# Batch 1's values loaded in two halves around q and k of batch 2, and batch 2's first transposes moved up

## The chip, the cores and the metric

The kernel runs on one core of a Trainium2 chip. The core has five engines, each with its own instruction stream: TensorE (PE; its weight loads are listed apart as PEld), VectorE (DVE), ScalarE (ACT), GpSimd (POOL) and SyncE (SP). They meet only at semaphores. Transfers between DRAM and the on-chip memory are done by 16 DMA engines; POOL and SP issue nearly all of them here, and the instructions of the engines arrive by DMA too. The metric is device time in microseconds (us), the median of several runs. The kernel before takes 302.07 us (three runs, 301.28 to 302.17).

## What is computed

Global-local attention for 8 batches of 8 heads, 512 local and 32 global tokens with head dimension 64, and then a two-layer network on the 4352 resulting rows of 512 numbers:

```python
s_g = scale * q_g @ concat(k_g, k_l).T
out_g = softmax(s_g) @ concat(v_g, v_l)
s_ll = where(abs(i - j) <= 32, scale * q_l @ k_l.T, -1e9)
s_lg = scale * q_l @ k_g.T
out_l = softmax(concat(s_lg, s_ll)) @ concat(v_g, v_l)
x = concat(out_g, out_l)          # per batch and head, then heads side by side: [4352, 512]
h = x @ w_in                      # [512, 2048]
out = (h * sigmoid(1.702 * h)) @ w_out
```

All inputs and the output are float32; the kernel casts to bf16 as it loads.

## The kernel before

*Tiling.* Heads are worked on four at a time. Such a group is a "quad": batch b has quads 2b (heads 0 to 3) and 2b + 1 (heads 4 to 7). In the code around the change `a` is the first quad of a batch and `c` the second. Local tokens are laid out as 16 by 32 positions. The local scores of a quad are computed for five overlapping chunks of keys (`PARTS`, `FIRST`), in two rounds (`rnd` 0 and 1), each round filling a pair of PSUM tiles from `spair()`.

*Steps of a quad* (class `Wide`, on top of `Quad`). `Tk` and `Tq` turn the loaded k and q (tiles `rk` and `rq` in `loaded[b]`) by a VectorE transpose into `kT` and `q`. `kcopy` and `qcopy` make second copies of parts of them. `ext` puts the global q and k next to the local ones; its four parts can run on VectorE, or on ScalarE if `on_act` is given. `transpose_g` turns the global q and k of some quads. `S(rnd)` is the score product on TensorE (L557), `X(rnd)` the exponential on ScalarE (L568), `M(rnd)` the product with the band mask (L573), on VectorE unless POOL is given. `U(0)` sums the exponentials through a matrix of ones, `U(1)` and `U(2)` multiply them with the two halves of the values (L583), `Gm` does the global rows (L594). `R` turns the sums and takes reciprocals (L459 to L463), `XL` scales and writes `xL`, the input of the network (L468), and `G` finishes the global rows.

*The network.* `h_mm` is the first product (L612, 64 matmuls of 512 columns a batch), `h_act` the activation: tanh on ScalarE (L619) and one VectorE instruction (L620) that writes `gT`. For four of the sixteen tiles of batch 1 this goes in two pairs (L829, L830). `o_mm` is the second product (L637); every fourth one ends in `o_out`, which copies PSUM to `ob` on ScalarE (L651) and stores it by four DMAs from SP (L659).

*Order.* The schedule is written out by hand: each engine executes its instructions in the order of the program text. The program does batch 0's attention, then batch 0's first product, then (L763 on) the second product of batch 0 with batch 1's attention strewn in, then batch 1's first product (L811 to L855), then `phase_o(1)`, the second product of batch 1 with the rest of batch 2's attention, and so on in the same pattern for batches 2 to 7. Batch 2's quad `a` is prepared during batch 1's first product: its transposes, copies and `ext` at `fc` 1 to 6, its first scores at `fc` 10.

*Loads.* Nearly all loads are issued by POOL, in program order, between POOL's own work. `load_rest` (L250) issues the values of batch 0, the weights, q and k of batch 1, and at its end the values of batch 1 (`load_v(1)`, five DMAs, one for each chunk of keys, over all eight heads), half of q of batch 2 and the global q and k of quads 4 to 7 (`load_g(4, 8)`). Then POOL does `a.M(0)` of batch 1 (L775), issues all of k and the other half of q of batch 2 (L776, L777), does `c.M(0)` (L789) and issues the values of batch 2 and q and k of batch 3. Eight semaphores serve POOL's loads in turn, so each issue waits until the load eight places earlier has landed. The global rows of batch 1's values are loaded once (`load_vg1`) and copied to three more places on ScalarE by `copy_vg1` (L105; L778).

*Names.* L is the line number. `loaded[2][0]` is k and `loaded[2][1]` q of batch 2; the second index `[:, u]` takes one quad's half.

Of the kernel before, what the change touches and what calls it, by code (L numbers as in the profile page):

```python
# [20 lines left out]
def kernel(  # L21
# [12 lines left out]
    nc = tc.nc  # L34

    B, H, Sl, D = q_l.shape
# [29 lines left out]
    qf = q_l.rearrange("b (u j) (r t) d -> b (j r) u (t d)", j=4, t=16)  # L66
    kf = k_l.rearrange("b (u j) (r t) d -> b (j r) u (t d)", j=4, t=16)
# [4 lines left out]
    loaded = {}  # L72

    def load(b, us=(0, 1), kq=True):
        if b not in loaded:
            loaded[b] = (ld.tile([128, 2, 16 * D], BF16, name="rk"),
                         ld.tile([128, 2, 16 * D], BF16, name="rq"))
        if kq:
            s = slice(us[0], us[-1] + 1)
            nc.gpsimd.dma_start(out=loaded[b][1][:, s], in_=qf[b][:, s])  # L80
            nc.gpsimd.dma_start(out=loaded[b][0][:, s], in_=kf[b][:, s])
# [3 lines left out]
    FIRST = (0, 96, 192, 320, 416)  # L85

    def v_view(b, n):
        return vtiles[b % 2][:, : 8 * n * (D + 2)].rearrange("p (u j c d) -> p u j c d", u=2, j=4, c=n)

    def load_v(b):  # L90
        if b == 2:
            nc.gpsimd.memset(v_view(b, 5)[:, :, :, :, D:], 1.0)
        vt = v_view(b, 5).rearrange("p u j c d -> p (u j) c d")
        vs, vg = (x[b].rearrange("h s d -> s h d") for x in (v_l, v_g))
        for c in range(5):
            n = 128 if c == 2 else 96
            nc.gpsimd.dma_start(out=vt[0:n, :, c, :D], in_=vs[FIRST[c] : FIRST[c] + n])  # L97
            if c != 2 and b != 1:
                nc.gpsimd.dma_start(out=vt[96:128, :, c, :D], in_=vg)  # L99

    def load_vg1():
        vt = v_view(1, 5).rearrange("p u j c d -> p (u j) c d")
        nc.gpsimd.dma_start(out=vt[96:128, :, 0, :D], in_=v_g[1].rearrange("h s d -> s h d"))

    def copy_vg1():  # L105
        vt = v_view(1, 5).rearrange("p u j c d -> p (u j) c d")
        src = vt[96:128, :, 0:1, :D]
        on_act(vt[96:128, :, 1:2, :D], src)
        on_act(vt[96:128, :, 3:5, :D], src.to_broadcast([32, 8, 2, D]))

    def on_act(out_, in_):
        nc.scalar.activation(out_, in_, AF.Copy)  # L112
# [11 lines left out]
    def load_g(lo, hi, names="kq"):  # L124
        for name, dst, src in (("k", rkg, kgf), ("q", rqg, qgf)):
            if name in names:
                nc.gpsimd.dma_start(out=dst[:, lo:hi, :], in_=src[:, lo:hi, :])
# [37 lines left out]
    for i in range(2):  # L165
# [3 lines left out]
        out=step, in_=step, pattern=[[1, 289]], compare_op=ALU.is_ge,  # L169
# [51 lines left out]
    def make_mask(part):  # L221
        rnd, at, t0, t1, nr, base, rows = part
        src = band[:, base : base + 16 * nr].rearrange("p (r t) -> p t r", t=16)
        nc.gpsimd.tensor_copy(mask_at(rnd, at, t1 - t0, nr)[0:rows], src[0:rows, t0:t1])
# [13 lines left out]
    def transpose_g(lo, hi, names="qk"):  # L238
        for name, dst, s in (("q", qgT, rqg), ("k", kgT, rkg)):
            if name not in names:  # L240
                continue
            nc.vector.transpose(dst[:, lo:hi, :32], s[:, lo:hi].bitcast(F32))

    def load_v2(b):
        vp = v_l[b].rearrange("(u h) (c p) d -> u p h c d", u=2, p=128)
        for u in range(2):
            for p in (slice(0, 64), slice(64, 128)):
                nc.gpsimd.dma_start(out=v_view(b, 4)[p, u, :, :, :D], in_=vp[u, p])

    def load_rest():  # L250
        load_v2(0)
        n = d_ff // 4
        for part in range(4):
            if part == 3:
                for m in MASKS:
                    make_mask(m)
            for u in range(2):
                nc.gpsimd.dma_start(out=w_in_sb[:, part, 2 * u : 2 * u + 2],
                                    in_=w_in_r[u][:, :, part * n : part * n + n])
        for g4 in (1, 0, 2, 3):  # L260
            nc.gpsimd.dma_start(
                out=w_out_sb[:, 4 * g4 : 4 * g4 + 4, :].rearrange("p (g e) m -> p g (e m)", e=2),
                in_=w_out_r[:, 2 * g4 : 2 * g4 + 2, :])
            if g4 == 0:
                load(1, (0,))
                load_g(2, 4)
                load_vg1()
            if g4 == 2:
                load(1, (1,))
        load_v(1)  # L270
        load(2, kq=False)
        nc.gpsimd.dma_start(out=loaded[2][1][:, 0], in_=qf[2][:, 0])
        load_g(4, 8)

    xG = consts.tile([128, NKC, B * Sg], BF16)
    xL = {}
# [328 lines left out]
    def width(i):  # L605
        return TB if i < B else B * Sg
# [3 lines left out]
    def h_mm(i, fc, hp, kcs):  # L610
        for kc in kcs:
            nc.tensor.matmul(hp[:, : width(i)], lhsT=w_in_c[:, fc // 4, kc, fc % 4 // 2, :, fc % 2],  # L612
                             rhs=(xL[i] if i < B else xG)[:, kc, :],
                             start=(kc == 0), stop=(kc == NKC - 1))

    def h_act(i, fc, hp):
        n = width(i)
        th = moe.tile([128, TB], F32, name="th", bufs=4)
        nc.scalar.activation(th[:, :n], hp[:, :n], AF.Tanh, scale=0.851)  # L619
        nc.vector.scalar_tensor_tensor(gTs[i][:, fc, :n], in0=th[:, :n], scalar=1.0,  # L620
                                       in1=hp[:, :n], op0=ALU.add, op1=ALU.mult)

    def h_step(i, fc):
        if fc == 0:
            gTs[i] = moe.tile([128, FC, TB], BF16, name="gT")
        hp = pbank("hp")
        h_mm(i, fc, hp, range(NKC))
        h_act(i, fc, hp)

    def o_mm(i, st):  # L630
        tci, f4 = divmod(st, 4)
        first = (i, tci) not in ops
        if first:
            ops[i, tci] = pbank("op")
        op = ops[i, tci]
        for fc in range(4 * f4, 4 * f4 + 4):
            nc.tensor.matmul(op, lhsT=gTs[i][:, fc, tci * 128 : tci * 128 + 128],  # L637
                             rhs=w_out_sb[:, fc, :], start=(first and fc == 4 * f4), stop=(fc == FC - 1))
        if f4 == 3:
            o_out(i, tci, op)  # L640
# [27 lines left out]
    a, c = Quad(0), Quad(1)  # L668
# [90 lines left out]
    def osteps(i, *sts):  # L759
        for tci, f4 in sts:  # L760
            o_mm(i, 4 * tci + f4)

    nq = {1: (Wide(2), Wide(3)), 2: (Wide(4), Wide(5))}  # L763
    a, c = nq[1]
    transpose_g(2, 4)
    a.Tk(False)
    a.Tq(False)
# [4 lines left out]
    osteps(0, (0, 1), (0, 0), (1, 1), (1, 0), (2, 1), (2, 0))  # L772
    a.S(0)
    a.X(0)
    a.M(0, nc.gpsimd)  # L775
    nc.gpsimd.dma_start(out=loaded[2][0], in_=kf[2])  # L776
    nc.gpsimd.dma_start(out=loaded[2][1][:, 1], in_=qf[2][:, 1])  # L777
    copy_vg1()  # L778
    c.Tk()
    c.Tq()  # L780
    c.ext()
    osteps(0, (0, 2), (1, 2), (2, 2))
    a.S(1)
    a.X(1)
    a.M(1)
    osteps(0, (0, 3), (1, 3))
    c.S(0)
    c.X(0)
    c.M(0, nc.gpsimd)  # L789
    load_v(2)  # L790
    load(3)
    osteps(0, (2, 3), (3, 0))
    c.S(1)
    c.X(1)
    for unit in range(3):
        a.U(unit)
    a.R()
# [15 lines left out]
    for kcs in ((0, 1), (2,), (3,)):  # L813
        for fc in range(4):
            h_mm(1, fc, hps[fc], kcs)
    a.G()
    c.G()
    pt = spair()
# [3 lines left out]
    a, c = nq[2]  # L822
    for fc in range(FC):
        if fc < 4:
            h_act(1, fc, hps[fc])
        elif fc in (4, 6):
            f = slice(fc, fc + 2)
            th, ps = early[:, fc - 4 : fc - 2], pt[1 - (fc - 4) // 2]
            nc.scalar.activation(th, ps, AF.Tanh, scale=0.851)  # L829
            nc.vector.scalar_tensor_tensor(gTs[1][:, f, :], in0=th, scalar=1.0, in1=ps,  # L830
                                           op0=ALU.add, op1=ALU.mult)
        elif fc >= 8:
            h_step(1, fc)
        if fc == 1:
            transpose_g(4, 6)
            a.Tk(False)
        if fc in (2, 3):
            a.ext((fc - 2,), on_act)
        if fc == 3:
            a.Tq(False)  # L840
        if fc == 4:
            a.kcopy(on_act)
            a.ext((2,), on_act)
        if fc == 6:
            a.ext((3,), on_act)
            a.qcopy(on_act)
        if fc == 10:
            a.S(0)
            a.X(0, (0,))
        if fc == 11:  # L850
            a.X(0, (1,))
            a.M(0, nc.gpsimd)
            load_v(3)
            load(4)
            load_g(8, NQ)  # L855
# [109 lines left out]
```

## Time and profile before

| what | value |
|---|---|
| median of three runs | 302.07 us |
| the profiled execution | 303.67 us, of which 302.0 us from the first to the last instruction (the span) |
| mean granted TensorE clock | 0.994 of full speed |
| one batch in the regular part (from batch 2 to batch 3) | 33.0 us |
| second product of batch 0 with batch 1's attention | 32.3 to 55.0 us |
| first product of batch 1 | 55.0 to 72.4 us |
| bytes moved by DMA, mean rate | 28.19 MB, 93 GB/s |
| DMA rate in 20 to 40 us / 65 to 75 us | 202 / 3 GB/s |

How to read the lines of the profile: an instruction's row has engine, line, operation, the tiles it writes and reads, the shapes, and the count. In a timeline the first number is the start, the second the length, both in us, and the bracket says how long the engine stood idle ahead of it and what released it; "issue" means that nothing the profile shows held it. In the chain of waits the two numbers are start and length of each piece. A DMA issue is listed with its size and the time from issue to landing. "DMA queue" rows give packets, MB and share of the 16 engines' time; q0 holds POOL's loads, q1 SP's stores, q8 and q14 carry instructions.

### The profile page before, as it was taken

What the parts mean: (1) busy time and instruction counts of PE and PEld (TensorE: products, weight loads), DVE (VectorE), ACT (ScalarE), POOL (GpSimd) and SP (SyncE); (2) the same over time, 40 slices, a digit from 0 to 9 for tenths busy, and PEclk for the clock granted to TensorE, in tenths of its full rate; (3) what the DMA queues carried; (4) which work ended last, traced back from release to release, by engine and by line L of the source; (5) the groups of instructions that cost most, each with busy time, mean ns of one, the idle gap of its engine ahead of it and who ended that gap; (6) DMA issues with size and microseconds to landing.
All of it is one profiled execution on the core that took longest, in us unless ns stands there. A gap on an engine that the chain in (4) does not pass through costs nothing.

```text
span 302.0 us, 8148 instructions
## 1 busy us (share of the span) xinstructions
PE 288.5 (96%) x3390; PEld 150.2 (50%) x3431; DVE 215.0 (71%) x421; ACT 173.1 (57%) x284; POOL 87.1 (29%) x131
## 2 busy tenths in 40 slices
PE   6999999799999999999999999999999999999995
PEld 6544445244554455444554455445454455446653
DVE  7678756498777878797887878797969866673320
ACT  4836695089556764476537746577357651663421
POOL 8973779607927000810054001600000000000000
PEclk9999999799999999999999999999999999999999
DMA  7999999950999711990269512900220012101113
GB/s 200 172 196 211 205 163 186 178 104 4 145 199 155 130 28 45 112 175 14 61 77 135 99 37 72 123 1 20 55 54 17 2 41 67 35 0 37 36 47 94
DMA packets 59444, 28.19 MB, mean 93 GB/s; under 512 B 47504, under 2 KB 49808, under 8 KB 59408
## 3 DMA queue, kind: packets, MB, share of 16 engines
q0 software_dynamic: 51568, 17.57, 52.6%
q1 hardware_dynamic: 7360, 9.45, 11.4%
q10 hardware_dynamic: 480, 0.66, 0.7%
q8 instruction: 27, 0.44, 0.6%
q14 instruction: 9, 0.07, 0.1%
HBM read 36.31 MB, written 8.91 MB: 150 GB/s over the span
## 4 chain that ended last, share of the span: by engine, by line
PE 85%; ACT 4%; DVE 3%; issue 2%; ACTq 0%
PE hp L612 36%; PE op L637 35%; PE ov L583 5%; PE s L557 5%; ACT e L568 2%; PE s L612 1%; DVE gT L620 1%; ACT ob L651 1%; DVE gT L830 1%; PE op L649 1%; PE og L594 1%; ACT v L112 1%; PE s L583 0%; DVE e L573 0%; DVE kT L509 0%
## 5 line engine op out<-in xcount | busy, mean ns | idle before, releaser
L637 PE MATMUL op<-w_out_sb,gT 128*128 128x512 bf16 x498 | 119.1, 379 | 2.4 <-DVE rT L461 0.7
L620 DVE SCALAR_TENSOR_TENSOR gT<-th,hp 128x512 bf16<-128x512 f32 (+1 forms) x136 | 86.8, 654 | 38.2 <-ACT th L619 38.2
L612 PE MATMUL hp<-xL,w_in_sb 128*128 128x512 bf16 x471 | 106.3, 383 | 0.6 <-issue 0.2
L619 ACT ACTIVATE th<-hp 128x512 f32<-128x512 f32 (+1 forms) x136 | 77.1, 573 | 44.7 <-PE hp L612 41.9
L612 PEld LDWEIGHTS <-w_in_sb 128*128 128x128 bf16 x576 | 56.4, 99 | 65.3 <-issue 2.4
L637 PEld LDWEIGHTS <-gT 128*128 128x128 bf16 x528 | 49.3, 98 | 55.7 <-issue 0.8
L651 ACT ACTIVATE ob<-op 128x512 f32<-128x512 f32 (+2 forms) x35 | 20.4, 588 | 66.0 <-PE op L637 63.5
L568 ACT ACTIVATE e<-s 128x1016 bf16<-128x1016 f32 (+1 forms) x56 | 53.5, 1006 | 2.0 <-PE s L557 1.9
L97 POOL DMA_DIRECT2D v<-in_v_l_dram x35 | 28.3, 815 | 82.3 <-PE og L594 81.5
L573 DVE TENSOR_TENSOR e<-e,mask 128x1712 bf16<-128x1712 bf16 (+1 forms) x25 | 27.1, 1082 | 6.0 <-ACT e L568 5.4
L459 DVE STREAM_TRANSPOSE sT<-ov 128x512 f32<-128x512 f32 x15 | 10.8, 717 | 19.5 <-PE ov L583 18.0
L468 DVE TENSOR_TENSOR xL<-ov,rs 128x512 bf16<-128x512 f32 x29 | 18.7, 685 | 1.8 <-PE ov L435 0.5
L557 PEld LDWEIGHTS <-kT 32*128 32x128 bf16 x672 | 12.8, 93 | 13.2 <-issue 9.7
L557 PE MATMUL s<-q,kT 32*128 32x160 bf16 (+1 forms) x448 | 15.0, 246 | 0.8 <-DVE gT L830 0.5
L509 DVE STREAM_TRANSPOSE kT<-rk 128x512 f32<-128x512 f32 x14 | 14.6, 1039 | 1.6 <-DMA rk<-in_k_l_dram 1.6
L99 POOL DMA_DIRECT2D v<-in_v_g_dram x24 | 14.3, 595 | 0.3 <-DMA v<-in_v_g_dram 0.3
L573 POOL TENSOR_TENSOR e<-e,mask 128x1760 bf16<-128x1760 bf16 x3 | 10.0, 3322 | 12.9 <-issue 12.2
L463 DVE STREAM_TRANSPOSE rs<-rT 128x512 f32<-128x512 f32 x16 | 11.4, 711 | 0.6
L583 PEld LDWEIGHTS <-v 128*32 128x32 bf16 x672 | 10.5, 97 | 2.4 <-issue 2.4
L583 PE MATMUL ov<-e,v 128*32 128x128 bf16 (+3 forms) x624 | 11.7, 223 | 0.0
L314 DVE STREAM_TRANSPOSE q<-rq 128x512 f32<-128x512 f32 (+1 forms) x17 | 11.2, 662 | 0.0
L612 PE MATMUL hp<-xG,w_in_sb 128*128 128x256 bf16 x64 | 9.6, 273 | 0.0
(112 smaller groups left out, 182.4 us busy)
## 6 DMA issues: line engine op xcount, KB each, us to landing
out_dram<-ob SPq DMA_DIRECT2D x132, 64.0 KB, 2.3
rk<-in_k_l_dram POOLq DMA_DIRECT2D x6, 512.0 KB, 9.6
v<-in_v_l_dram POOLq DMA_DIRECT2D x28, 96.0 KB, 4.7
rq<-in_q_l_dram POOLq DMA_DIRECT2D x5, 512.0 KB, 7.5
w_in_sb<-in_moe_w_in_dram POOLq DMA_DIRECT2D x8, 256.0 KB, 7.6
w_out_sb<-in_moe_w_out_dram POOLq DMA_DIRECT2D x4, 512.0 KB, 10.1
v<-in_v_l_dram POOLq DMA_DIRECT2D x11, 128.0 KB, 4.8
rq<-in_q_l_dram POOLq DMA_DIRECT2D x5, 256.0 KB, 9.0
```

The costliest lines, as they stand in the source:

```text
L97: nc.gpsimd.dma_start(out=vt[0:n, :, c, :D], in_=vs[FIRST[c] : FIRST[c] + n])
L468: nc.vector.tensor_mul(self.x[:, 2 * self.u + h, :], self.st[1 + h], self.st["rs"])
L509: nc.vector.transpose(flat[:, 0:Sl].rearrange("p (r t) -> p t r", t=16), loaded[self.b][0][:, self.u].bitcast(F32))
L557: nc.tensor.matmul(bank(self.ps, j)[:, at : at + n], lhsT=self.k[p, KEYS[c] : KEYS[c] + 128, e], rhs=qs[p, :, :, e], start=(e == 0), stop= ...
L568: nc.scalar.activation(self.E[rnd][:, 2 * i : 2 * i + 2, :n], self.ps[i][:, :, :n], AF.Exp, scale=scale)
L573: eng.tensor_mul(e, e, mask[:, rnd : rnd + 1, :n].to_broadcast([128, 4, n]))
L583: nc.tensor.matmul(ov[32 * j : 32 * j + 32, :].rearrange("p (t r) -> p t r", t=16)[:, t0:t1, r0 : r0 + nr], lhsT=lv, rhs=self.E[rnd][:, j, ...
L612: nc.tensor.matmul(hp[:, : width(i)], lhsT=w_in_c[:, fc // 4, kc, fc % 4 // 2, :, fc % 2], rhs=(xL[i] if i < B else xG)[:, kc, :], start=( ...
L619: nc.scalar.activation(th[:, :n], hp[:, :n], AF.Tanh, scale=0.851)
L620: nc.vector.scalar_tensor_tensor(gTs[i][:, fc, :n], in0=th[:, :n], scalar=1.0, in1=hp[:, :n], op0=ALU.add, op1=ALU.mult)
L637: nc.tensor.matmul(op, lhsT=gTs[i][:, fc, tci * 128 : tci * 128 + 128], rhs=w_out_sb[:, fc, :], start=(first and fc == 4 * f4), stop=(fc = ...
L651: nc.scalar.activation(ob[:, lo:hi], op[:, lo:hi], AF.Copy, scale=0.5)
```

## The change

`load_v` takes a range of heads. The values of batch 1 are loaded in two calls, heads 0 to 3 and heads 4 to 7 (ten DMAs of half the size in place of five). Between them stand q and k of quad 4 (the first half of batch 2) and the global q and k. The other half of q and k of batch 2 is issued after `c.M(0)` of batch 1, ahead of the values of batch 2. `a.M(0)` of batch 1 moves from POOL to VectorE and behind the preparation of `c`. `copy_vg1` moves to the start of batch 1's attention. The transposes of quad 4 (`Tq`, `Tk`) move into batch 1's attention behind `a.M(1)`, its `kcopy` and `qcopy` behind `c.X(1)`, and the global transposes ahead of `a.G()`. In batch 1's first product there remain the four parts of `ext`, one behind each of the first four tiles. The order of TensorE's instructions is the same as before.

```diff
--- before.py
+++ after.py
@@ -87,14 +87,14 @@
     def v_view(b, n):
         return vtiles[b % 2][:, : 8 * n * (D + 2)].rearrange("p (u j c d) -> p u j c d", u=2, j=4, c=n)
 
-    def load_v(b):
+    def load_v(b, hs=slice(0, 8)):
         if b == 2:
             nc.gpsimd.memset(v_view(b, 5)[:, :, :, :, D:], 1.0)
         vt = v_view(b, 5).rearrange("p u j c d -> p (u j) c d")
         vs, vg = (x[b].rearrange("h s d -> s h d") for x in (v_l, v_g))
         for c in range(5):
             n = 128 if c == 2 else 96
-            nc.gpsimd.dma_start(out=vt[0:n, :, c, :D], in_=vs[FIRST[c] : FIRST[c] + n])
+            nc.gpsimd.dma_start(out=vt[0:n, hs, c, :D], in_=vs[FIRST[c] : FIRST[c] + n, hs])
             if c != 2 and b != 1:
                 nc.gpsimd.dma_start(out=vt[96:128, :, c, :D], in_=vg)
 
@@ -267,10 +267,10 @@
                 load_vg1()
             if g4 == 2:
                 load(1, (1,))
-        load_v(1)
-        load(2, kq=False)
-        nc.gpsimd.dma_start(out=loaded[2][1][:, 0], in_=qf[2][:, 0])
+        load_v(1, slice(0, 4))
+        load(2, (0,))
         load_g(4, 8)
+        load_v(1, slice(4, 8))
 
     xG = consts.tile([128, NKC, B * Sg], BF16)
     xL = {}
@@ -762,6 +762,7 @@
 
     nq = {1: (Wide(2), Wide(3)), 2: (Wide(4), Wide(5))}
     a, c = nq[1]
+    copy_vg1()
     transpose_g(2, 4)
     a.Tk(False)
     a.Tq(False)
@@ -772,26 +773,28 @@
     osteps(0, (0, 1), (0, 0), (1, 1), (1, 0), (2, 1), (2, 0))
     a.S(0)
     a.X(0)
-    a.M(0, nc.gpsimd)
-    nc.gpsimd.dma_start(out=loaded[2][0], in_=kf[2])
-    nc.gpsimd.dma_start(out=loaded[2][1][:, 1], in_=qf[2][:, 1])
-    copy_vg1()
     c.Tk()
     c.Tq()
     c.ext()
+    a.M(0)
     osteps(0, (0, 2), (1, 2), (2, 2))
     a.S(1)
     a.X(1)
     a.M(1)
+    nq[2][0].Tq(False)
+    nq[2][0].Tk(False)
     osteps(0, (0, 3), (1, 3))
     c.S(0)
     c.X(0)
     c.M(0, nc.gpsimd)
+    load(2, (1,))
     load_v(2)
     load(3)
     osteps(0, (2, 3), (3, 0))
     c.S(1)
     c.X(1)
+    nq[2][0].kcopy(on_act)
+    nq[2][0].qcopy(on_act)
     for unit in range(3):
         a.U(unit)
     a.R()
@@ -813,6 +816,7 @@
     for kcs in ((0, 1), (2,), (3,)):
         for fc in range(4):
             h_mm(1, fc, hps[fc], kcs)
+    transpose_g(4, 6)
     a.G()
     c.G()
     pt = spair()
@@ -831,19 +835,8 @@
                                            op0=ALU.add, op1=ALU.mult)
         elif fc >= 8:
             h_step(1, fc)
-        if fc == 1:
-            transpose_g(4, 6)
-            a.Tk(False)
-        if fc in (2, 3):
-            a.ext((fc - 2,), on_act)
-        if fc == 3:
-            a.Tq(False)
-        if fc == 4:
-            a.kcopy(on_act)
-            a.ext((2,), on_act)
-        if fc == 6:
-            a.ext((3,), on_act)
-            a.qcopy(on_act)
+        if fc < 4:
+            a.ext((fc,), on_act)
         if fc == 10:
             a.S(0)
             a.X(0, (0,))
```

## The prediction, made before the change was run

> **What bounds the kernel now.** I read the page first, then the chain that ended last around the stage that the change touches, then the busy time in windows there.
>
> ```profile
> PE 288.5 (96%) x3390; PEld 150.2 (50%) x3431; DVE 215.0 (71%) x421; ACT 173.1 (57%) x284; POOL 87.1 (29%) x131
> q8 instruction: 27, 0.44, 0.6%
> out_dram<-ob SPq DMA_DIRECT2D x132, 64.0 KB, 2.3
> ```
>
> TensorE is busy for 96% of the span, so the change cannot gain by making anything else faster; it can only remove idle or slow time of TensorE. The second row is the DMA queue that carries instructions: 27 packets for 3390 + 3431 = 6821 TensorE instructions, about 253 instructions a packet. The third is what a store of the output takes on the whole from issue to landing: 2.3 us.
>
> The chain between 40 and 75 us holds one wait far longer than the others:
>
> ```profile
> 51.54 0.94 PE s L583 x62
> 52.48 2.23 issue
> 54.71 0.35 PE s L583 x10
> ```
>
> This is `c.U` of batch 1 (quad 3), the last attention products ahead of batch 1's h matmuls. For 2.23 us TensorE waits, and no semaphore explains it ("issue"). What had it just done? The tile view of the value tile, up to 52.4 us, says:
>
> ```profile
> L583 PE MATMUL s<-e,v x38: 195/218/249, 51.7 to 52.3; 128*32 128x128 bf16 x12, 128*32 128x192 bf16 x12, 128*32 128x120 bf16 x8, 128*32 128x72 bf16 x6
> ```
>
> Two units have eight matmuls of 72 columns; six were done. The stop lies inside a group of four that read the same chunk of the values and the same scores. No data wait falls there: TensorE had run out of instructions. The DMA views confirm it. First 43.3 to 52.25 us, then 52.25 to 53.3 us:
>
> ```profile
> q0 software_dynamic: 1433, 0.98, 89.8%
> q1 hardware_dynamic: 311, 0.44, 16.4%
> q14 instruction: 1, 0.01, 0.2%
> issues: line engine op xcount, KB each, median us to landing
> out_dram<-ob SPq DMA_DIRECT2D x12, 64.0 KB, 6.3
> rk<-in_k_l_dram POOLq DMA_DIRECT2D x1, 512.0 KB, 6.6
> rq<-in_q_l_dram POOLq DMA_DIRECT2D x1, 256.0 KB, 9.0
> ```
>
> ```profile
> q8 instruction: 1, 0.02, 5.7%
> ```
>
> No packet of q8 in the first stretch, one right behind it. The first stretch is filled by k of batch 2 (512 KB, issued at 44.58) and half of its q (256 KB, issued at 45.32, down 9.0 us later). The stores issued in it took 6.3 us instead of 2.3: whatever was put on the engines then waited behind those 768 KB, and I take it that the instruction packet did too. When was it asked for?
>
> ```profile
> 4.80:8.20 3.40, 1.86 (x57) 1.73 (x58) 2.69 (x11) 1.26 (x2) 3.40 (x6) 1.00 1.10 244
> 48.00:50.00 2.00, 1.84 (x35) 1.00 (x25) 1.93 (x4) 1.08 (x2) 2.00 (x3) 1.00 1.15 175
> 50.00:52.30 2.30, 2.30 (x108) 1.57 (x106) 2.30 (x4) 0.60 (x1) 2.30 (x5) 1.00 1.02 227
> 52.56:55.97 3.41, 1.21 (x14) 0.65 (x15) 1.94 (x5) 0.00 (x0) 3.15 (x5) 1.00 1.96 198
> 55.97:59.38 3.41, 3.41 (x9) 1.18 (x8) 1.60 (x7) 0.00 (x0) 2.00 (x3) 0.50 1.75 177
> ```
>
> The columns after the stretch are PE, PEld, DVE, ACT and POOL, the granted clock, DMA share and GB/s. Counting back one packet of 253 from the stop, 214 instructions lie in 50.0 to 52.3 and the other 39 bring us to about 48.7 us: an estimate of the request, if it is made one packet ahead. The last row is the second price: right after the stop the clock was 0.50 for 3.41 us, so 1.70 us of matmul time were lost. The stretch before it, in which TensorE was busy 1.21 of 3.41 us, is the likely reason; the first row shows a stretch with 1.86 of 3.40 after which the clock stayed at 1.00.
>
> **The change, part by part.** *The loads.* POOL's queue before, and landings of single issues:
>
> ```profile
> 32.39 4.00 POOL L97 DMA_DIRECT2D v<-in_v_l_dram x5 [0.54 <-DMA rk<-in_k_l_dram]
> 36.86 0.56 POOL L272 DMA_DIRECT2D rq<-in_q_l_dram x1 [0.47 <-DMA rq<-in_q_l_dram]
> 38.09 0.75 POOL L127 DMA_DIRECT2D rkg<-in_k_g_dram x1 [0.67 <-DMA rk<-in_k_l_dram]
> 40.55 0.74 POOL L127 DMA_DIRECT2D rqg<-in_q_g_dram x1 [1.71 <-DMA w_out_sb<-in_moe_w_out_dram]
> 46.61 3.32 POOL L573 TENSOR_TENSOR e<-e,mask 128x1760 bf16<-128x1760 bf16 x1 [0.72 <-ACT e L568]
> ```
>
> ```profile
> rqg<-in_q_g_dram POOLq DMA_DIRECT2D x1, 64.0 KB, 5.3
> ```
>
> ```profile
> DMA to landing us min/median/max: 2.6/4.8/9.0
> ```
>
> Each issue waits for the landing of the one eight issues before it (q of batch 2 for q of batch 1, rqg for the third quarter of w_out). The same rule on the new order gives: five half pieces of the values from 32.39, q of quad 4 at 36.86, k of quad 4 at 38.09 (what stood eighth before it is the same), the two global loads from 40.55 to 42.0, then the second five half pieces. A full piece costs 0.80 us of POOL (4.00 / 5); taking that as the upper bound, POOL is through at 46.0, in time for `c.M(0)` at 46.6. The bytes ahead of and including rqg are the same as before: half of the values (256 KB) is replaced by half of k (256 KB), so these loads are down when rqg was, 40.55 + 5.3 = 45.9. The second half of the values is 256 KB more. The last piece lands 2.6 (shortest) to 9.0 us (longest) after 46.0; with a queue that empties at about 45.9 and 256 KB at some 175 GB/s (1.5 us), I take the short end, 48.6. `c.Gm` is the first to read it:
>
> ```profile
> 51.03 0.51 PE L594 MATMUL s<-v,e 128*32 128x66 bf16 x40
> ```
>
> That leaves 2.4 us; at the long end (55.0) it would be a stall of its own, the rival below.
>
> The rest of q and k of batch 2, the values of batch 2 and all of batch 3 are now behind `c.M(0)`, so they are issued from 46.61 + 3.32 = 49.9 on. Between the landing near 48.6 and 49.9 the queue is empty but for stores. A request near 48.7 is then served at once. So the stall goes: **minus 2.23**, and with it the half clock: **minus 1.70**. Bounds of this pair: 0 and 3.93; the value is the full end, because the 768 KB that stood in front are gone from there. What is late next on POOL: two issues of 0.56 us stand ahead of the values of batch 2 and of load 3, 1.1 us. Their readers come after 72 us (the transposes of quad 5 at 73.2, `U` of quad 4 at 76.6, batch 3 at 81.8), all over 10 us behind even with 9.0 us for landing and 4 us less time. Cost nothing.
>
> *ScalarE.* `copy_vg1` moves from behind `a.X(0)` to the front.
>
> ```profile
> 34.70 0.52 ACT L112 ACTIVATE q<-qgT 128x128 bf16<-128x128 bf16 x2 [1.55 <-DVE qgT L242]
> 40.24 1.57 ACT L112 ACTIVATE v<-v 32x512 bf16<-32x512 bf16 x2
> 41.83 1.89 ACT L568 ACTIVATE e<-s 128x992 bf16<-128x992 f32 x2
> ```
>
> ```profile
> v<-in_v_g_dram POOLq DMA_DIRECT2D x1, 32.0 KB, 9.2
> ```
>
> Its 1.57 us fit into the idle 1.55 us ahead of 34.70; its source, issued at 23.64, is down at 32.8. If it came late, `ext`, `kcopy` and `qcopy` behind it, and so `a.S(0)`, would wait. Taken out at 40.24, it lets `a.X(1)` follow `a.S(1)`, which ends at 41.5: 0.3 us sooner, and all later exponentials with it. What that can buy is bounded by TensorE's two waits for them and by zero:
>
> ```profile
> PE s L557 <- ACT e L568: 0.4, 2, 0.2
> ```
>
> I take **minus 0.3**.
>
> *VectorE.* It gains `a.M(0)` and the two transposes of quad 4 in this stage and loses the latter in the next.
>
> ```profile
> 43.82 1.74 DVE L573 TENSOR_TENSOR e<-e,mask 128x1712 bf16<-128x1712 bf16 x1 [3.30 <-ACT e L568]
> 47.73 0.72 DVE L459 STREAM_TRANSPOSE sT<-ov 128x512 f32<-128x512 f32 x1 [2.17 <-PE ov L583]
> 55.10 1.29 DVE L468 TENSOR_TENSOR xL<-s,rs 128x512 bf16<-128x512 f32 x2 [1.40 <-PE s L583]
> 61.82 1.02 DVE L509 STREAM_TRANSPOSE kT<-rk 128x512 f32<-128x512 f32 x1
> 63.87 0.68 DVE L314 STREAM_TRANSPOSE q<-rq 128x512 f32<-128x512 f32 x1
> 80.88 1.03 DVE L573 TENSOR_TENSOR e<-e,mask 128x1760 bf16<-128x1760 bf16 x1
> ```
>
> `a.M(0)` costs 1.03 where POOL took 3.3; it fits into the 3.30 idle us ahead of 43.82. The transposes, 1.02 + 0.68 = 1.70, fit into the 2.17 ahead of 47.73 if k of quad 4 is down by 45.9 as worked out; then they end by 47.0. `a.M(0)` waits for `a.X(0)` with nothing urgent behind it. If k came 9.0 us after 38.09, at 47.1, `a.R` would begin 0.4 us late and the products behind it could hold the h matmuls by as much: bounds 0 to plus 0.5, value nothing. With the stall gone the 1.40 idle us at 55.10 go too, and the last `xL` ends about when the h matmuls that need it come up; that is cover with little to spare, inside the same bound.
>
> *The h stage of batch 1.* The 0.43 us of global transposes move to a place where VectorE is idle; `kcopy` and `qcopy` (0.36 + 0.53) leave ScalarE there for its idle time after `c.X(1)`. The wait at stake:
>
> ```profile
> 66.85 0.53 PE L557 MATMUL s<-q,kT 32*128 32x160 bf16 x16 [0.50 <-DVE gT L830]
> ```
>
> ScalarE now does four tanh and four copies before its two wide tanh, so the wide products end hardly sooner. Bounds: plus 0.3 (copies ahead of the tanh) and minus 0.5; I take **minus 0.15**.
>
> Sum: 2.23 + 1.70 + 0.3 + 0.15 = 4.4 us. The profiled execution took 303.67 us (span 302.0): it would become 299.3. The median of the runs is 302.07, 1.6 below it: **297.7**.
>
> **Rivals.** *The packet does not wait behind loads.* Then moving them leaves stall and clock as they are: 302.07 - 0.45 = 301.6. For it: nothing in the trace shows a request. Against it: its start right at the end of the q load and the stores' 6.3 us. The Trainium skill speaks for it: DMA: Bandwidth & Descriptors, section Queues, rings and completion order, says that each DMA engine takes turns between the queues that have work, a packet at a time; by that the instruction packet would have waited for little, and the time would be this rival's. The trace's 6.3 us for stores on another queue do not agree.
>
> *A short stall stays*, because stores and the tail of the values are still there: up to 1.5 us, below the idle time that left the clock at 1.00 in the row of 4.80 to 8.20. 297.7 plus 1 = 298.7, at most 299.2.
>
> *The clock drops anyway.* Only the 2.23 and the small terms go: 299.4. Against it, the clock is 1.00 before the stop. The Trainium skill, TensorE: Matmul & The Clock Gate, section Part 1: The HAM clock gate, ties the drop to an idle window of about 3.4 us; by its letter a gap of 2.23 us would not suffice and the drop would have another cause, so the sum would be 299.4. The measured 0.50 straight behind the gap decides for me.
>
> *The other side:* the second half of the values lands late. From 46.0 with the 9.0 us of the longest row it is down at 55.0; `c.Gm`, now at 50.7, stops for 4.3 us and the clock drops, against 2.23 before: 302.07 + 2.1 - 0.45 = 303.7. It decides against the change from a landing at about 53.5 on. Against it: the long landings had 768 KB in front.
>
> **How the numbers follow.** Forecast 0.60; short stall 0.12; clock 0.06; packet unmoved 0.10; late values 0.10; a gain over the sum 0.02. Range: below, 302.07 - (2.23 + 1.70 + 0.4 + 0.5) = 297.2, and 0.4 for the spread of the runs, 296.8; above, the clock case with the 0.5 of VectorE, 299.9, and a bit of spread, 300.3. A measurement of this kernel tells about 0.3%, 0.9 us, from no change. Faster: 0.80; same: 0.10; slower: 0.10.
>
> **What would show it.** Right: no "issue" wait near 52 us, clock 1.00 through 50 to 60 us, q8's packet starting near 49; h matmuls of batch 1 from about 52.5; then the same steps some 4 us sooner. `a.M(0)` on VectorE at about 40.5 for 1.03; the transposes of quad 4 before 47.7. Wrong: TensorE or POOL waiting on a load of v; a new "issue" wait; `a.R` behind the k of quad 4.

## The result and the profile after

The changed kernel takes 299.66 us (six runs, 298.40 to 300.09) against 302.11 us for the kernel before in the same comparison (six runs, 301.28 to 303.09): a ratio of 0.9914, 95% interval 0.9888 to 0.9939. The forecast was 297.7, with a range of 296.8 to 300.3. The profiled execution of the changed kernel took 299.75 us, with a span of 298.0; before it was 303.67 with 302.0. So the two profiles differ by 3.9 us and the two medians by 2.45: this gap is the main thing to explain.

First TensorE's timeline of the changed kernel at the place of the old stall (start, length, count, and in brackets the idle time ahead):

```profile
51.57 0.91 PE L583 MATMUL s<-e,v 128*32 128x128 bf16 x48
52.42 1.90 PE L612 MATMUL hp<-xL,w_in_sb 128*128 128x512 bf16 x7
54.47 1.89 PE L612 MATMUL hp<-xL,w_in_sb 128*128 128x512 bf16 x8 [0.16 <-DVE xL L468]
```

All 48 matmuls of the two units run through, and the h matmuls of batch 1 begin at 52.42, not at 54.99. The instruction packet, in the DMA view of 48.6 to 48.7 us:

```profile
q8 instruction: 1, 0.02, 76.9%
```

It begins in that tenth of a microsecond, where it began at 52.3 before. (The share is of 16 engines over the window: 0.769 x 16 x 0.1 = 1.23 us for this packet.) The windows, with PE, PEld, DVE, ACT, POOL and the granted clock after each stretch:

```profile
50.00:52.30 2.30, 2.30 (x117) 1.62 (x115) 2.30 (x4) 0.60 (x1) 2.30 (x5) 1.00 0.64 68
52.30:55.70 3.40, 3.19 (x27) 1.39 (x15) 3.16 (x9) 0.00 (x0) 3.40 (x6) 1.00 1.05 180
55.70:59.00 3.30, 3.30 (x17) 1.47 (x15) 3.23 (x8) 3.25 (x9) 1.66 (x3) 1.00 1.99 204
```

The clock stays at 1.00. POOL and VectorE around it:

```profile
42.56 3.43 POOL L97 DMA_DIRECT2D v<-in_v_l_dram x5
46.53 3.33 POOL L573 TENSOR_TENSOR e<-e,mask 128x1760 bf16<-128x1760 bf16 x1 [0.54 <-ACT e L568]
```

```profile
40.97 1.07 DVE L573 TENSOR_TENSOR e<-e,mask 128x1760 bf16<-128x1760 bf16 x1
46.47 1.09 DVE L509 STREAM_TRANSPOSE kT<-rk 128x512 f32<-128x512 f32 x1 [1.12 <-DMA rk<-in_k_l_dram]
47.58 0.72 DVE L459 STREAM_TRANSPOSE sT<-ov 128x512 f32<-128x512 f32 x1
```

POOL was through with the values at 46.0 as forecast. What was not forecast is the wait that TensorE has left. The waits of TensorE between 40 and 80 us that changed (in total, times, longest), before and after; two rows of 0.2 us that stand in both are left out:

```profile
PE s L583 <- issue: 2.2, 1, 2.2
PE op L637 <- DVE rT L461: 0.7, 1, 0.7
PE s L557 <- DVE gT L830: 0.5, 1, 0.5
PE s L557 <- ACT e L568: 0.4, 2, 0.2
```

```profile
PE op L637 <- DVE rs L463: 1.2, 1, 1.2
PE s L557 <- ACT e L568: 0.2, 1, 0.2
PE hp L612 <- DVE xL L468: 0.2, 1, 0.2
```

The account of the two profiles closes: 2.23 (stall), 1.70 (half clock), 0.25 (0.43 to 0.18, waits for the exponentials) and 0.50 (wait for the wide products) are gone; 0.16 (`xL`, above) and 0.53 (0.67 to 1.20 at `op`, near 73.5 us) have come. That is 4.0 us, the difference of the spans.

### The profile page after: what moved, and what is told of

It is laid out like the page before. It is cut to its first block, busy times and chain, and to the rows that moved or that the text cites. A ratio compares the mean times of both kernels' runs of the same rounds, so it can differ in the third digit from the quotient of the medians.

```text
span 298.0 us, 8159 instructions
## 1 busy us (share of the span) xinstructions
PE 287.4 (96%) x3390; PEld 150.2 (50%) x3431; DVE 216.2 (73%) x422; ACT 173.6 (58%) x284; POOL 86.9 (29%) x136
## 4 chain that ended last, share of the span: by engine, by line
PE 86%; DVE 3%; ACT 2%; issue 2%; ACTq 0%; DVEq 0%
PE hp L612 36%; PE op L637 36%; PE s L557 5%; PE ov L583 5%; PE s L612 2%; ACT e L568 2%; ACT ob L651 1%; PE op L649 1%; DVE rs L463 1%; DVE sT L459 1%; DVE xL L468 1%; PE og L594 1%; DVE e L573 0%; PE ov L420 0%; PE ov L435 0%
## 5 line engine op out<-in xcount | busy, mean ns | idle before, releaser
L612 PE MATMUL hp<-xL,w_in_sb 128*128 128x512 bf16 x471 | 104.8, 379 | 0.7 <-issue 0.2
L97 POOL DMA_DIRECT2D v<-in_v_l_dram x40 | 30.9, 776 | 84.5 <-PE og L594 82.2
L463 DVE STREAM_TRANSPOSE rs<-rT 128x512 f32<-128x512 f32 x16 | 11.4, 711 | 0.6
L557 PE MATMUL s<-qc,kT 32*128 32x120 bf16 (+1 forms) x224 | 8.0, 212 | 0.2 <-ACT e L568 0.2
```

The lines of the kernel that those rows point to most:

```text
L97: nc.gpsimd.dma_start(out=vt[0:n, hs, c, :D], in_=vs[FIRST[c] : FIRST[c] + n, hs])
L557: nc.tensor.matmul(bank(self.ps, j)[:, at : at + n], lhsT=self.k[p, KEYS[c] : KEYS[c] + 128, e], rhs=qs[p, :, :, e], start=(e == 0), stop= ...
```

## The experiments

Two theories stood at the start. One: the stall is an instruction packet that arrives late, and the half clock behind it comes by chance. The other: the moved copies and transposes brought the gain. All times are medians; the kernel before ran beside each group (301.79, 301.61 and 302.05 us).

**The kernel before once more.**

> The kernel before, unchanged, for the span and granted clock of each run. Theory 1 (the stall comes every time, the half clock only sometimes): the runs fall into two groups, span near 302 with clock 0.994 and span near 300.3 with clock 1.00, and the second is the more frequent, so that the median is 302.1 although the profiled execution took 303.7. Rival (the half clock comes every time and the profiled execution was slow for another reason): all runs show 0.994. The stall near 52.5 us in the profile: 2.2 us by both.

Measured: 301.69 us (12 runs, 300.76 to 305.25; ratio 1.0003, 0.9966 to 1.0039). Over all the runs of the kernel before beside these experiments, 81 with this one, 24 have a granted clock of 0.994 or less and a median of 303.93, and 57 have 0.997 or more and a median of 301.55; their ranges overlap (301.54 to 305.85 and 300.26 to 302.55). A clock of 0.994 is what one stretch of 3.4 us at half clock leaves in 302 us. So such a stretch is a matter of chance, in three runs of ten; where it lay in those runs is known only where a profile was taken. This profile is of the frequent kind; TensorE and the clock:

```profile
54.23 0.35 PE L583 MATMUL s<-e,v 128*32 128x72 bf16 x10 [1.54 <-issue]
```

```profile
54.20:60.00 5.80, 5.72 (x35) 2.69 (x36) 4.31 (x13) 1.94 (x5) 3.70 (x6) 1.00 1.80 190
```

The stall is there at the same matmul, 1.54 us this time, and the clock behind it is 1.00. The span is 299.8 us, 2.2 under the profile that the prediction was made from and 1.8 over that of the changed kernel.

**The loads and the mask product.**

```diff
+        load_v(1, slice(0, 4))
+        load(2, (0,))
         load_g(4, 8)
+        load_v(1, slice(4, 8))
...
-    a.M(0, nc.gpsimd)
-    nc.gpsimd.dma_start(out=loaded[2][0], in_=kf[2])
-    nc.gpsimd.dma_start(out=loaded[2][1][:, 1], in_=qf[2][:, 1])
...
     c.ext()
+    a.M(0)
...
     c.M(0, nc.gpsimd)
+    load(2, (1,))
```

> The kernel before with the new load order and a.M(0) on VectorE (it cannot stay on POOL, where it would now queue behind the second half of the values); copy_vg1 and batch 2's transposes stay where they were. Theory (the stall is an instruction packet behind k and q of batch 2): no unexplained wait near 52 us, clock 1.00, median 299.7 to 300.2, that is nearly all of the change's gain. Rival (the gain came from the moved transposes and copies): the stall stays and the median is 301.5 or more.

Measured: 300.39 us (299.17 to 301.24; ratio 0.9945, 0.9918 to 0.9972). No unexplained wait near 52 us; the wait at `op`, near 74 us, is 0.88 us in this profile. The gain is over half of the change's, not nearly all of it.

**The mask product alone.**

```diff
-    a.M(0, nc.gpsimd)
...
     c.ext()
+    a.M(0)
```

> The kernel before with a.M(0) on VectorE alone. POOL then issues the 768 KB of k and q some 3 us sooner, from about 41.5 us. Theory (the packet waits for what is queued in front of it at 48.4 us): the 768 KB are through on the faster engines at about 48 to 49.5, the packet arrives before TensorE runs dry at 52.1, no stall or one under 0.7 us, median 299.7 to 300.5. Rival (it is the order of the bytes or the number of loads, not when they are issued): the stall stays at 2 us and the median at 301.5 to 302.

Measured: 300.53 us (299.08 to 302.09; ratio 0.9957, 0.9933 to 0.9981). With this one move there is no stall in the profile: k and half of q are issued 2.8 us sooner than before (44.58 and 45.32), and the values' matmuls of the two units run through.

```profile
41.76 0.71 POOL L775 DMA_DIRECT2D rk<-in_k_l_dram x1
42.50 0.57 POOL L776 DMA_DIRECT2D rq<-in_q_l_dram x1
```

```profile
53.07 0.91 PE L583 MATMUL s<-e,v 128*32 128x128 bf16 x48
```

The order of the loads is not what mattered here; what mattered is when they were issued, with no POOL product of 3.3 us in front of them. This profile has its half clock at another place, at the start:

```profile
9.56:12.97 3.41, 3.32 (x29) 1.66 (x32) 1.47 (x6) 2.98 (x7) 3.35 (x6) 0.50 2.09 159
```

So the clock can drop there too, and a granted clock of 0.994 alone does not say that the stall was the cause. A later start and this drop brought TensorE to the place of the stall 1.3 us later than in the first profile (53.07 against 51.73), which gave the packet more time. That the move alone is enough is therefore shown better by the run with 31 dummy matmuls further down, where TensorE is there at 51.91 and does not stop. The wait at `op` has grown to 1.47 us in this profile.

**Where the blocks of instructions end.** If TensorE runs dry at the end of a block of its instruction stream, dummy matmuls at the start, where it waits for the first loads, move every later stop.

```diff
-    fill(21, psP.tile([128, 512], F32, name="w", tag="p"), True)
+    fill(31, psP.tile([128, 512], F32, name="w", tag="p"), True)
```

> The changed kernel with 31 in place of 21 dummy matmuls at the very start, where TensorE waits for the first loads: every later instruction of TensorE stands 20 places further along in its stream. Theory (the wait of 1.2 us at 73.5 us, which the profile puts down to VectorE, is an instruction packet that comes late after 218 instructions of small matmuls): the wait shrinks to about 0 to 0.7 us or moves by 20 instructions, median 298.8 to 299.5. Rival (it is VectorE's reciprocal step, L463): the wait stays at 1.2 us at the same matmul.

Measured on the changed kernel: 298.34 us (six runs, 298.27 to 298.39; ratio 0.9887, 0.9852 to 0.9922). The wait of 1.2 us is gone, and so is the spread. The same place in both, first the changed kernel, then with the shift:

```profile
73.13 0.33 PE L594 MATMUL og<-v,e 128*32 128x66 bf16 x20
74.67 1.68 PE L637 MATMUL op<-w_out_sb,gT 128*128 128x512 bf16 x6 [1.20 <-DVE rs L463]
```

```profile
73.06 0.33 PE L594 MATMUL og<-v,e 128*32 128x66 bf16 x20
73.33 2.97 PE L637 MATMUL op<-w_out_sb,gT 128*128 128x512 bf16 x12
```

VectorE's `rs` (L463) comes at the same time in both, and with the shift TensorE goes on before it has begun:

```profile
73.60 0.71 DVE L463 STREAM_TRANSPOSE rs<-rT 128x512 f32<-128x512 f32 x1
```

So "DVE rs" was never the reason. In the changed kernel the packet began in 71.7 to 71.8 us and took 0.940 x 16 x 0.1 = 1.50 us:

```profile
q8 instruction: 1, 0.02, 94.0%
```

It ended at 73.2 to 73.3, and TensorE went on 1.4 us later, at 74.67. A second run of this kernel:

> The changed kernel with 31 dummy matmuls once more, beside the three above on one chip: 298.2 to 298.5, all runs within 0.3.

Measured: 298.58 us (298.20 to 299.23; ratio 0.9872, 0.9831 to 0.9914). The wait near 73.5 us is absent again; the spread of 1.0 us is not what was expected, and its reason is open. And with twice the shift:

> The changed kernel with 41 dummy matmuls, a shift of 40 places. Theory (where the blocks of the instruction stream end decides): no wait at 73.5 us, as with a shift of 20; other block ends fall elsewhere in the later batches, and one of them may now fall at the end of a stretch of small matmuls (near 150 or 177 us) and cost up to 1 us: median 298.0 to 299.4. Rival (dummy matmuls help by warming the clock): the more the better, 297.5 to 298.3.

Measured: 298.32 us (four runs, 298.25 to 298.73; ratio 0.9885, 0.9839 to 0.9930), the same as with half of it: no warming that adds up, and no new stall.

**The other way, in the kernel before.**

```diff
-    fill(21, psP.tile([128, 512], F32, name="w", tag="p"), True)
+    fill(9, psP.tile([128, 512], F32, name="w", tag="p"), True)
-    fill(8, a.bk[1][3])
```

> The kernel before with 20 dummy matmuls fewer (9 in place of 21, and the 8 further down left out): a shift by 40 places the other way. The loads stand as before. Theory: TensorE reaches the end of its block 20 matmuls later, in the wide h matmuls, some 2.5 us later, while the packet is asked for 0.4 us later: the stall of 1.5 to 2.2 us near 52.5 us goes or falls under 0.5 us, and the one of 0.6 us near 76 too: median 299.0 to 300.3, if the colder start costs under 0.5 us. Rival (the stall is some wait of the attention step itself): it stays, 301.5 or more.

Measured: 300.87 us (12 runs, 300.02 to 301.79; ratio 0.9964, 0.9940 to 0.9988), 0.6 over what was expected. TensorE's waits between 50 and 80 us, all of them:

```profile
PE s L557 <- DVE gT L829: 0.5, 1, 0.5
```

Both stalls are gone with not a load moved, and none of the 12 runs has a clock under 0.997. Part of it is given back ahead of this place: the values' matmuls of `c.U` start at 53.11 us, 1.4 us later than in the first profile of the kernel before (51.73). All of that has come by 13 us, while the same matmuls of the first scores take longer (355 ns on average, not 292), which fits a colder start. The later arrival gives the packet time as well, so this run alone does not show that the place of the block end decides; the next two do.

**Loads put in front of the packet**, in the changed kernel with 31 dummy matmuls; the second of the two runs moves q of batch 3 up as well.

```diff
+    load(2, (1,))
     c.M(0, nc.gpsimd)
-    load(2, (1,))
     load_v(2)
```

> The changed kernel with 31 dummy matmuls (as in the run of the shift by 20), and q and k of quad 5 (512 KB) issued ahead of c.M(0), not behind it, so that they stand in the queue when the instruction packet is asked for at about 48.2 us. Theory (the packet waits for what is in front of it): it starts at about 50.2 in place of 48.4, arrives at about 52.7 to 53, TensorE runs dry at about 52.0: a stall of 0.6 to 1.2 us at the 234th matmul pair or so after the start of c.U, median 298.9 to 299.6. Rival (the packet takes turns with the loads, one packet each): no stall, 298.3 as without.

> As the run with 512 KB, with q of batch 3 (512 KB more) also ahead of c.M(0). Theory: each 512 KB put 2.5 us in front of the packet, which starts at about 52.8: a stall of 3 to 3.8 us at the same place, most often with a stretch of half clock behind it, median 301.3 to 303.5. Rival: no stall, 298.3 to 298.6 (c.M(0) ends 0.7 us later).

Measured: 299.99 us (299.49 to 302.51; ratio 0.9954, 0.9923 to 0.9984) and 300.25 us (299.51 to 303.06; 0.9954, 0.9920 to 0.9988), where the shift alone had 298.3. TensorE with 512 KB, then with 1024 KB:

```profile
51.91 0.28 PE L594 MATMUL s<-v,e 128*32 128x66 bf16 x12 [0.64 <-DVE e L573]
52.38 0.59 PE L583 MATMUL s<-e,v 128*32 128x128 bf16 x28
53.21 0.49 PE L583 MATMUL s<-e,v 128*32 128x192 bf16 x20 [0.24 <-issue]
```

```profile
52.32 0.59 PE L583 MATMUL s<-e,v 128*32 128x128 bf16 x28
53.38 0.49 PE L583 MATMUL s<-e,v 128*32 128x192 bf16 x20 [0.48 <-issue]
```

The stop is back, and it comes after 28 matmuls, where it came after 38 in the kernel before: ten matmuls earlier, which with their weight loads are the 20 instructions of the shift. That fixes it as the end of a block. The wait at `op` fits this: in the kernel before, 734 weight loads stand ahead of the first stop and 988 ahead of the one at `op`, and 254 weight loads with their matmuls are 508 instructions, two packets. The packet began in 50.75 to 50.85 us with 512 KB, against 48.4 in the same kernel without the move, and in 51.0 to 51.1 with 1024 KB. So the first 512 KB put 2.4 us in front of it and the second 512 KB almost nothing. The stall is smaller than expected in both, 0.24 for 0.6 to 1.2 and 0.48 for 3 to 3.8 us; but both profiles are of executions among the fastest of their ten (299.49 and 299.55 us). The second lot was issued about a microsecond ahead of the request; whether it was too late to be in front, the runs do not tell. Part of the loss has another reason: `c.M(0)` starts later and holds up VectorE's `c.M(1)` (the 0.64 us, and 0.95 with 1024 KB).

**What each part is worth without the stalls.** Three kernels with 31 dummy matmuls: the mask product alone; it and the new load order; it and `copy_vg1` moved, with the old order.

> The kernel before with a.M(0) on VectorE and 31 dummy matmuls, nothing else; the load order of before. Theory (the loads need no new order, only no mask product of POOL in front of them): no stall at 52 and none at 75 us, little spread, 299.0 to 299.4, which is the run below within 0.3. Rival (the new order is worth something of its own): 299.8 or more, with runs at a clock of 0.994.

> The same with the new load order. Theory: 299.0 to 299.3, the same as with the old order; both 0.7 to 0.9 above the changed kernel with its 31 dummy matmuls (298.3), for TensorE's waits of 0.4 (exponentials) and 0.5 us (wide products) that copy_vg1 and batch 2's transposes take away. Rival: 0.5 or more under the run above.

> The run with a.M(0) on VectorE, 31 dummy matmuls and the old load order, and copy_vg1 at the start of batch 1's attention in addition. Theory: TensorE's two waits for ScalarE's exponentials (0.25 and 0.18 us) shrink to one of about 0.18, median 0.2 to 0.4 below the run without, 298.7 to 299.0. Rival (the copy was not on the path): the same as without.

Measured: 299.27 us (299.08 to 299.52), 299.17 (298.80 to 299.38) and 298.87 (298.61 to 299.62), with ratios 0.9894 (0.9853 to 0.9935), 0.9889 (0.9848 to 0.9930) and 0.9882 (0.9836 to 0.9927). The new load order is worth 0.1 us beside the mask product, less than the runs spread. `copy_vg1` is worth 0.4, and what is left of the change 0.3 (to 298.58, in the same comparison). In that last step a part may be a stall, for the third of these kernels shows what the new order is still good for:

```profile
51.55 0.60 PE L583 MATMUL s<-e,v 128*32 128x128 bf16 x28
52.95 0.49 PE L583 MATMUL s<-e,v 128*32 128x192 bf16 x20 [0.80 <-issue]
```

With the old order the stall can come back, 0.80 us, once TensorE reaches the block end a little sooner (0.36 us, by the start of these matmuls); in the profiles with the new order and `load(2, (1,))` behind `c.M(0)` it is absent.

The granted clock goes the same way. Six of the kernels show neither stop in their profile (dummy matmuls 31, twice, 41 and 9; the mask product alone and with the new order at 31), and none of their 40 runs has a clock under 0.997. With the stops there, it is 0.994 or less in 24 of 81 runs of the kernel before, in 5 of 20 with loads put in front at 31 dummy matmuls, in 7 of 24 of the two early experiments (the mask product, alone and with the loads), and in one of six of the changed kernel. That the stops bring the half clock is likely by this, but it is not shown run by run.

## Why the prediction was right, and where it was off

*The stall* (minus 2.23). Right in mechanism: TensorE ran dry of instructions, and the packet stood behind k and q. Shown by the stop that moves with the instruction stream, by its going when the loads come sooner, and by its return with 512 KB put back. The rival "the packet does not wait behind loads" falls. One reading was loose: the packet did not start "right at the end of the q load". That load was down at 54.3 (45.32 + 9.0), and the packet began at 52.3. The trace has 16 landings for this load, the first at 52.2 and 15 of them by 53.0. This fits a packet that stands behind one engine's share of the loads and not behind the last byte; on which engine it was, the trace does not say. The size of the stall varies, 1.54 us in the other profile of the kernel before.

*The half clock* (minus 1.70). This is the term that was mis-sized. The prediction read it off one execution and took it to be in the median as well. In 57 of 81 runs of the kernel before there is no such stretch, so the median contains little of it: 301.73 over all 81, 301.55 over the 57. The row of 303.67 us beside a median of 302.07 was the sign: the profiled execution had something that most do not have, and the 1.6 us between them were carried over as if they were fixed. Against the profile the sum was good: 299.3 forecast, 299.75 measured. For the medians 4.4 us were forecast and 2.45 came; that 299.66 still lies in the range, near its upper end, is owed to the bound for "the clock drops anyway" (299.4 and 0.5). That rival comes close to the measured time by another road: here the clock stays at 1.00 after the change, and mostly it had not dropped before.

*ScalarE* (minus 0.3): the waits fell from 0.43 to 0.18 us, and the pair of runs gives 0.4. *The h stage* (minus 0.15): the whole 0.50 went; the bound was right and the value too small. It goes only with the transposes moved: it is there in all five runs with `a.M(0)` on VectorE and the transposes where they were.

*VectorE* (0): k of quad 4 came later than worked out, its transpose began at 46.47 and ended just as `sT` was due, at 47.58. The cover was used up, and nothing was lost by it: the 0.16 us at `xL` are there (0.15) in the runs of the mask product alone and of the loads with it, where the transposes are not moved. *The late values* (rival): POOL was done at 46.0 as forecast, and the first reader, `c.Gm`, did not wait.

*What was not seen*: a second place of the same kind. The 0.67 us at `op` in the profile of before, put down to VectorE there, was already a late packet, and it grew to 1.20 us. This gave back 0.53 us. Ten more dummy matmuls take it away.

## What to carry to other kernels

A wait of TensorE without a releaser, in the middle of a group of matmuls that share their data, is a block of instructions that came late; add or drop dummy instructions ahead and see whether the stop moves by as many. Stretches of many small matmuls use up a block in 2 to 4 us (here 214 instructions in 2.3 us), so keep large loads out of the queue there, or let the block end fall among wide matmuls. And before a term is read off a profile, look at where this execution stands among the runs: a loss that comes in three runs of ten is no part of the median.

## What the runs showed of the hardware

One packet of instructions serves about 254 TensorE instructions (508 between the two stops) and takes 0.9 to 1.6 us in the first profile of the kernel before. After it ends, TensorE takes some time more to go on: 1.4 us at 73.2 to 74.67, and 1.0 to 1.4 us in the ten stops that the profiles show at the two places. The Trainium skill, Runtime: NRT & Kernel Launch, section Instruction fetch mechanics, gives blocks of 16 KiB or 256 instructions, which agrees with 27 packets for 6821 instructions, and calls the cost of crossing a block mostly hidden; at these two places, where the matmuls are small, it is 0.24 to 2.23 us when the packet is late. The releaser that the profile names can be wrong in such a place: "DVE rs" stood for a late packet.

One program shows both: a stall of 2.23 us with 3.4 us of half clock behind it, and a stall of 1.54 us at the same matmul with none. The half clock begins at 55.97, 1.3 us after TensorE has gone on. The length of the idle time alone does not decide, as one place near the start shows, first in the profile of the kernel before, then in that of the mask product alone:

```profile
7.46 1.25 PE L353 MATMUL s<-q,kT 32*128 32x120 bf16 x48 [1.54 <-DVE q L314]
```

```profile
8.06 1.13 PE L353 MATMUL s<-q,kT 32*128 32x120 bf16 x44 [1.47 <-DVE q L314]
```

Behind the first the clock stays at 1.00, behind the second it is 0.50 from 9.56 to 12.97 us. What else decides, the runs do not tell.
